# Softmax attention beside linear attention on one core: three query chunks side by side, and VectorE's exponentials split by bit masks

## The chip, the cores and the metric

The kernel runs on one core of a Trainium2 chip. The metric is the device time of one launch, in microseconds (us). The engines have queues of their own: TensorE (PE; its weight loads are PEld), VectorE (DVE), ScalarE (ACT), GpSimd (POOL) and SyncE (SP), which here issues nearly all DMAs.

## The reference

The input is one sequence of 2048 rows of 1024 features in bf16. Two layers alternate, and the pair of them is applied twice with the same weights, each with a layer norm in front and a residual around it.

```python
def _A_ref(x, wqkv, w_phi, wo):          # linear attention, 32 heads of 32
    ...
    phi_q = jnp.concatenate([_softmax(pq, axis=-1), _softmax(-pq, axis=-1)], axis=-1)
    phi_k = jnp.concatenate([_softmax(pk, axis=-1), _softmax(-pk, axis=-1)], axis=-1)
    ...
def _B_ref(x, wqkv, wo):                 # softmax attention, 32 heads of 32
    ...
    scores = jnp.einsum("bhqd,bhkd->bhqk", q, k) * (Dh ** -0.5)
    p = _softmax(scores, axis=-1)
    o = jnp.einsum("bhqk,bhkd->bhqd", p, v)
    return (lambda x, *d: x.transpose(*d))(o, 0, 2, 1, 3).reshape(B, S, D) @ wo

x = A_x
x = x + _A_ref(_layernorm(x, axis=-1), A_wqkv, A_w_phi, A_wo)
x = x + _B_ref(_layernorm(x, axis=-1), B_wqkv, B_wo)
x = x + _A_ref(_layernorm(x, axis=-1), A_wqkv, A_w_phi, A_wo)
x = x + _B_ref(_layernorm(x, axis=-1), B_wqkv, B_wo)
```

The softmax layers hold most of the work: each has 32 heads x 2048 x 2048 scores, and every one needs an exponential.

## The kernel before

The kernel keeps x transposed in SBUF (`xT`, features on the partitions) and cuts the sequence into four chunks of 512 rows (`C512`, `NC` = 4). The 32 heads are eight groups of four (`G` = 8). A **turn** of a softmax layer is one query chunk with one head group, 32 turns a layer, listed in `turns`; `pos` gives a turn its number. Within a turn there are two halves (`pp`), each with 8 steps `d` and 4 score tiles `j`: 64 tiles of 128 keys x 512 queries.

The function `attention` takes these tiles three at a time. TensorE computes three scores side by side in different row groups (L1009) into three PSUM banks, and ScalarE makes one exponential of 1536 columns of them (L1017). TensorE then multiplies the probabilities with the values and with ones, the latter for the denominators: four small matmuls (L1047) per two tiles, accumulating in bank 6 (`acc`). VectorE copies the sum out (L1062). The denominators are gathered by small DMAs on SP (L1092), inverted on VectorE (L1097), written to DRAM (L1098) and read back spread over the heads (L1100), and VectorE scales the output (L1103).

Some tiles skip ScalarE. `exp_dve` takes a *pair* of tiles: two single score matmuls (L947) into bank 7, and then nine VectorE instructions that compute 2 to the power of the score. Each score is read twice from PSUM, once to round it with a large constant (L952) and once for the fraction (L955). Two steps over both tiles make the power of two out of the rounded value (L958, L961), three multiply-adds are a polynomial of the fraction (L966), and a last one multiplies (L969). `EXTRA` says which turns have which pairs.

Everything else of the softmax layers is fill, placed between the scores, in the single PSUM bank 7 (`FIL`), and copied out by VectorE: keys (`b_k`, L842 and the DMAs of L834), values (`b_v`), queries (`b_q`, L850, with two DMAs that swap halves of the partitions in `q_swap`, L855 and L856), the output projection (`b_o` in the first layer, `b_last` in the last), and in the first softmax layer also the key features of the linear layer that follows (`a_keys`). Projections in bank 7 run as four column groups (L428). Query chunks 2 and 3 are computed early and parked in DRAM (`q_away`, L866, L868) and fetched again before their turns (`q_back`, L874 to L876).

No engine order is written out by hand. A planner on the host, `Sched`, holds every operation with an engine, an estimated duration, its dependencies, its buffers and a priority that works as a due time. It plays the engines forward and puts the operations in order; the order is then fixed in the program, and on the chip each engine goes through its own list, waiting for semaphores. `QUOTA` limits how many buffers of a class are live. `base` and `at` are the due times of a layer and of its attention; a turn is 10 units. Where TensorE would be too idle, the planner inserts idle matmuls (L1265).

Of the kernel before, what the change touches and what calls it, by code (L numbers as in the profile page):

```python
# [19 lines left out]
DH = 32  # L20
# [27 lines left out]
class Sched:  # L48
# [96 lines left out]
    def run(self):  # L145
# [25 lines left out]
        while left:  # L171
# [86 lines left out]
         "e": 6, "vp": 6, "e1": 4, "vp1": 4, "E": 6, "q2": 3, "kt": 3, "w2": 8, "w2o": 3, "oT": 26, "T": 4, "den": 2,  # L258
         "lnt": 6, "lnw": 2, "lnw1": 1, "eq": 8, "ns": 4, "cw": 6, "hl": 6, "oc": 2, "slab": 7, "slabk": 3, "fin": 4,
         "rs": 8, "pkf": 1, "cden": 2, "part": 8, "w2r": 1,  # L260
         "xs": 1, "xu": 2, "xg": 2, "xx": 2, "E1": 3}
# [3 lines left out]
ROUND = 1.5 * 2**21  # L265
POW2_D = 0.32318750170670074
POW2_0 = 0.998010015430466
POW2_C = (-2.753493604392706, 3.611980637904819, -2.738565741928622)
LEAD = 5.0
EXTRA = (lambda i: [(0, 2), (1, 2)] if 12 <= i < 17 else [],  # L270
         lambda i: ([(0, 2), (1, 2)] if i % 3 else [(0, 2), (0, 5), (1, 4)]) if 16 <= i < 30 else [(i % 2, 2)] if 8 <= i < 16 else [])
# [14 lines left out]
def kernel(  # L286
# [20 lines left out]
    q_scale = float(DH**-0.5 / (4 * math.log(2)))  # L307
# [626 lines left out]
    def exp_dve(qc, g, pp, d, prio, kT, q_of):  # L934


        u_b, u_v = sb("xu", 2, C512, dt=F32)
        g_b, g_v = sb("xg", 2, C512, dt=F32)
        x_b, x_v = sb("xx", 2, C512, dt=F32)
        e_b, e_v = sb("E1", 2, C512)  # L940
        r = slice(96, 128)
        gs = []
        for k in range(2):
            s_b, s_v = ps("xs", FIL)

            def sfn(k=k, s_v=s_v):
                nc.tensor.matmul(  # L947
                    out=s_v(), lhsT=kT[g][1]()[r, pp, (d + k) * P:(d + k + 1) * P],
                    rhs=q_of[(qc, g)][1]()[r, (pp + 1) % 2, :], start=True, stop=True, tile_position=(96, 0))
            so = op("PE", MM, sfn, flat([kT[g][2][(d + k) // 2], q_of[(qc, g)][2]]),  # L950
                    [s_b, kT[g][0], q_of[(qc, g)][0]], prio, mode="r")
            uo = op("DVE", dve_us(512), lambda k=k, s_v=s_v: nc.vector.tensor_scalar(  # L952
                out=u_v()[:, k, :], in0=s_v(), scalar1=POW2_D, scalar2=ROUND, op0=ALU.add, op1=ALU.add),
                [so], [s_b, u_b], prio + 0.01)
            gs.append(op("DVE", dve_us(512), lambda k=k, s_v=s_v: nc.vector.scalar_tensor_tensor(  # L955
                out=g_v()[:, k, :], in0=u_v()[:, k, :], scalar=ROUND, in1=s_v(), op0=ALU.subtract, op1=ALU.subtract),
                [uo], [s_b, u_b, g_b], prio + 0.01))
        wo = op("DVE", 1024 / 1920 + 0.15, lambda: nc.vector.tensor_scalar(  # L958
            out=u_v(), in0=u_v(), scalar1=ROUND - 31.5, scalar2=ROUND + 32.0, op0=ALU.max, op1=ALU.min),
            gs, [u_b], prio + 0.02)  # L960
        wo = op("DVE", 1024 / 1920 + 0.15, lambda: nc.vector.tensor_scalar(  # L961
            out=u_v().bitcast(I32), in0=u_v(), scalar1=ROUND - 31.75, scalar2=float(2**25),
            op0=ALU.subtract, op1=ALU.mult), [wo], [u_b], prio + 0.02)
        last = gs
        for i, c in enumerate(POW2_C):
            last = [op("DVE", dve_us(1024), lambda i=i, c=c: nc.vector.scalar_tensor_tensor(  # L966
                out=x_v(), in0=(x_v() if i else g_v()), scalar=c, in1=g_v(), op0=ALU.add, op1=ALU.mult),
                last, [g_b, x_b], prio + 0.02)]
        eo = op("DVE", dve_us(1024), lambda: nc.vector.scalar_tensor_tensor(  # L969
            out=e_v(), in0=x_v(), scalar=POW2_0, in1=u_v(), op0=ALU.add, op1=ALU.mult),  # L970
            [wo, *last], [x_b, u_b, e_b], prio + 0.02)
        return eo, (e_b, lambda: e_v().rearrange("p a b -> p (a b)"))

    def attention(base, kT, vT, q_of, gate, extra):
# [7 lines left out]
        for qc, g in turns:  # L982
            for pp, d in extra(pos[(qc, g)]):
                eo, (e_b, e_v) = exp_dve(qc, g, pp, d, base + 10 * pos[(qc, g)] + 5 * pp + 0.5 * d - LEAD, kT, q_of)
                for k in range(2):
                    ex_of[(qc, g, pp, d + k, 3)] = eo
                    e_of[(qc, g, pp, d + k, 3)] = (e_b, e_v, k)
# [3 lines left out]
        while i < len(units):  # L991
# [14 lines left out]
            def sfn(grp=grp, s_v=s_v):  # L1006
# [11 lines left out]
                out=e_v()[:, 0:w * C512], in_=s_v(), func=ACT.Exp, scale=4 * math.log(2)),  # L1018
# [7 lines left out]
        if True:  # L1026
            for qc, g in turns:
                T = []
                end = (qc, g) == turns[-1]
                for pp in range(2):  # L1030
                    a_b, a_v = ps("acc", [(6,)])
                    last = None
                    for d in range(8):
                        prio = base + 10 * pos[(qc, g)] + 5 * pp + 0.5 * d
                        for u in range(2):
# [4 lines left out]
                            def fn(us=us, kc=kc, u=u, d=d, a_v=a_v, v_v=v_v, g=g, pp=pp):  # L1040
                                for k in range(2):
                                    eb, ev, x = e_of[us[k]]
                                    j = 2 * pp + k
                                    for what in range(2):
                                        col = 64 * ((pp + what) % 2) + 32 * k
                                        o = (g % 4) * P + j * DH
                                        nc.tensor.matmul(  # L1047
                                            out=a_v()[col:col + 32, :],
                                            lhsT=v_v()[:, kc % 4, o:o + DH] if what == 0 else ones_bf[:],
                                            rhs=ev()[:, x * C512:(x + 1) * C512],  # L1050
                                            start=(d == 0 and u == 0), stop=(d == 7 and u == 1),
                                            tile_position=(0, col), skip_group_check=True)
# [5 lines left out]
                            last.accum = (d, u) != (7, 1)  # L1058
# [53 lines left out]
    turns = [(qc, g) for g in range(G) for qc in range(2)] + [(qc, g) for qc in range(2, NC) for g in range(G)]  # L1112
    pos = {t: i for i, t in enumerate(turns)}
# [21 lines left out]
    for layer in range(2):  # L1135
        base = BASE[layer]
        second = base + (100, 45)[layer]
# [53 lines left out]
        for g in range(1, G):  # L1191
            pr = at + 10 * pos[(0, g)] - 19
            w = slab("w2", pr - 1, B_w[:, :, D + g * P:D + (g + 1) * P], P)
            for c in range(NC):
                b_k(g, c, pr + 4 * c, w, kT, FIL, "DVE")
        for c in range(NC):
            for t in range(TB):
                b_v(1, c, t, at + 4.5 * (4 * c + t) + 2, bv_s[1], vT, FIL, "DVE")
        for g in range(G):
            pr = at + 10 * pos[(0, g)]  # L1200
            w = slab("w2", pr - 11, B_w[:, :, g * P:(g + 1) * P], P) if g else wq0
            for qc in range(NC):
                if qc < 2:
                    if qc or g:
                        q_of[(qc, g)] = b_q(g, qc, pr + 10 * qc - 8, w, FIL)
                else:
                    away = q_away(g, qc, pr + 2 + 6 * (qc - 2), w, FIL)
                    q_of[(qc, g)] = q_back(g, qc, at + 10 * pos[(qc, g)] - 12, away)
        oTs, last_s = attention(at, kT, vT, q_of, gate, EXTRA[layer])
        if last:  # L1210
            bo_s = [slab("slab", at + 160 + fc, B_o[:, :, fc * C512:(fc + 1) * C512], C512) for fc in range(2)]
        for qc, p0, gap in ((0, 163, 1.5), (1, 176, 1.5), (2, 251, 1.5)):
            if last:
                gap = (6, 6, 9)[qc]
                p0 = (163, 200, 251)[qc]
# [85 lines left out]
```

## Time and profile before

| what | value |
|---|---|
| time, median of 3 runs | 2477.9 us (2477.84 to 2481.64) |
| span of the profiled execution | 2480.3 us, clock of TensorE 0.993 |
| the profiled execution's own time | not listed apart from the span; the span is 2.4 us above the median of the runs |
| first softmax layer's attention, first to last exponential of L1017 | about 358 to 1336 us |
| second one | about 1558 to 2468 us |
| ScalarE, L1017 | 1332 exponentials, 1798.9 us |
| VectorE busy | 1380.8 us, 538 of them between 1558 and 2481 us |
| pairs on VectorE | 10 in the first layer, 40 in the second |

A row of the profile names the line, the engine, the operation, what it writes and reads, the shape and the count; then the busy time, the mean of one in ns, and the engine's idle time before it with what ended that. ScalarE's exponentials overlap: one lasts 1.67 us, but in an unbroken run they start every 1.33 to 1.35 us, which is why 1332 of them are 1798.9 us busy. TensorE's matmuls overlap in the same way.

### The profile page before, as it was taken

Reading aid. Unit: us, or ns where it says so; the run is one execution under the profiler, and the core shown is the slowest. Engines: PE = TensorE matmul, PEld = TensorE weight load, DVE = VectorE, ACT = ScalarE, POOL = GpSimd, SP = SyncE. Lnnn points to the kernel's source line nnn. Section 1 sums busy time; section 2 is a strip of 40 time slices with the busy share of each in tenths; the row PEclk is TensorE's granted clock in tenths of the full one; section 3 lists DMA queues with packets and bytes.
Section 4 is the critical chain, followed back from the end, with each engine's and each line's share of the span. In section 5 each row is a group of like instructions: output and inputs, shape, how many; then the busy total and the mean of one; then the engine's idle time right before and its main releaser. Section 6 shows DMA issues by size and latency. Waiting matters only on the chain. (4 is left out here: it accounts for less than half of the span.)

```text
span 2480.3 us, 61740 instructions
## 1 busy us (share of the span) xinstructions
PE 2316.0 (93%) x27084; PEld 870.4 (35%) x27084; DVE 1380.8 (56%) x1947; ACT 2131.0 (86%) x1887; POOL 24.9 (1%) x72
## 2 busy tenths in 40 slices
PE   7999999999999999999889999999999999998998
PEld 4443443333333333333333444333333333333333
DVE  6997653222266634543535766322255568789863
ACT  6335548999999999999997455699999999999998
POOL 0000000000000000000000000000000000000000
PEclk9999999999999999999999999999999999999999
DMA  9020011111121122213324001111121110110000
GB/s 219 24 56 1 6 38 40 43 36 45 39 66 42 47 66 70 78 50 86 120 57 128 1 5 30 31 39 43 41 61 34 31 30 29 32 32 27 27 25 32
DMA packets 204373, 118.32 MB, mean 48 GB/s; under 512 B 122440, under 2 KB 194120, under 8 KB 203336
## 3 DMA queue, kind: packets, MB, share of 16 engines
q1 hardware_dynamic: 203048, 112.29, 16.7%
q8 instruction: 211, 3.46, 0.6%
q10 hardware_dynamic: 1056, 2.10, 0.3%
q14 instruction: 58, 0.48, 0.1%
HBM read 78.71 MB, written 16.24 MB: 38 GB/s over the span
## 5 line engine op out<-in xcount | busy, mean ns | idle before, releaser
L1017 ACT ACTIVATE arena<-psum 128x1536 bf16<-128x1536 f32 x1332 | 1798.9, 1670 | 38.1 <-PE psum L1009 29.3
L1047 PE MATMUL psum<-arena 128*32 128x512 bf16 x4096 | 656.2, 388 | 7.3 <-DVE arena L1062 5.8
L1047 PE MATMUL psum<-arena,ones_bf 128*32 128x512 bf16 x4096 | 656.3, 388 | 0.0
L1009 PE MATMUL psum<-arena 32*128 32x512 bf16 x3996 | 525.0, 384 | 99.5 <-ACT arena L1017 91.1
L428 PE MATMUL psum<-arena 128*32 128x512 bf16 x8256 | 575.5, 381 | 5.4 <-DVE arena L612 1.9
L424 PE MATMUL psum<-arena 128*128 128x512 bf16 x2032 | 473.4, 382 | 17.0 <-ACT arena L745 3.2
L1009 PEld LDWEIGHTS <-arena 32*128 32x128 bf16 x3996 | 176.9, 91 | 620.6 <-issue 607.1
L424 PEld LDWEIGHTS <-arena 128*128 128x128 bf16 x2032 | 192.5, 98 | 265.4 <-issue 48.2
L428 PEld LDWEIGHTS <-arena 128*32 128x32 bf16 x8256 | 201.9, 96 | 214.8 <-issue 68.4
L1047 PEld LDWEIGHTS <-arena 128*32 128x32 bf16 x4096 | 158.0, 95 | 269.4 <-issue 238.6
L842 DVE CAST arena<-psum 128x512 bf16<-128x512 f32 x112 | 77.2, 690 | 255.2 <-PE psum L428 249.2
L966 DVE SCALAR_TENSOR_TENSOR arena<-arena 128x1024 f32<-128x1024 f32 x150 | 183.3, 1222 | 7.1 <-PE psum L1047 2.8
L1265 PE MATMUL psum<-xT,zero 128*32 128x512 bf16 x2172 | 171.7, 382 | 0.0
L1047 PEld LDWEIGHTS <-ones_bf 128*32 128x32 bf16 x4096 | 155.2, 95 | 18.7 <-issue 8.3
L1062 DVE COPY arena<-psum 128x512 f32<-128x512 f32 x126 | 86.5, 687 | 88.2 <-PE psum L1047 86.8
L615 ACT ACTIVATE arena<-psum 128x512 bf16<-128x512 f32 x80 | 42.7, 601 | 86.9 <-PE psum L424 57.5
L1103 DVE TENSOR_TENSOR arena<-arena 64x512 bf16<-64x512 f32 x124 | 84.7, 683 | 51.8 <-DMA arena<-rd 42.5
L952 DVE TENSOR_SCALAR arena<-psum 128x512 f32<-128x512 f32 x100 | 68.8, 688 | 67.7 <-PE psum L947 61.5
L745 ACT ACTIVATE arena<-psum 128x512 bf16<-128x512 f32 x128 | 69.8, 598 | 41.8 <-PE psum L424 32.0
L619 DVE TENSOR_REDUCE arena<-arena 128x32 f32<-128x1024 bf16 x64 | 77.7, 1214 | 41.2 <-ACT arena L615 34.0
L513 DVE TENSOR_TENSOR arena<-xT,arena 128x1024 f32<-128x1024 bf16 x64 | 78.0, 1219 | 35.9 <-ACT arena L502 34.7
L628 DVE TENSOR_TENSOR arena<-psum,arena 128x1024 bf16<-128x1024 f32 x64 | 77.7, 1215 | 30.0 <-PE psum L428 25.0
(100 smaller groups left out, 1394.5 us busy)
## 6 DMA issues: line engine op xcount, KB each, us to landing
arena<-rd SPq DMA_DIRECT2D x62, 256.0 KB
arena<-in_A_wqkv_dram SPq DMA_DIRECT2D x10, 1024.0 KB
arena<-in_B_wqkv_dram SPq DMA_DIRECT2D x32, 256.0 KB
arena<-arena SPq DMA_DIRECT2D x256, 32.0 KB
arena<-in_B_wo_dram SPq DMA_DIRECT2D x32, 256.0 KB
arena<-wd_k SPq DMA_DIRECT2D x8, 1024.0 KB
arena<-in_A_wo_dram SPq DMA_DIRECT2D x4, 1024.0 KB
arena<-in_B_wqkv_dram SPq DMA_DIRECT2D x4, 1024.0 KB
```

The costliest lines, as they stand in the source:

```text
L424: nc.tensor.matmul(out_, lhsT=lhsT, rhs=rhs, start=start, stop=stop, skip_group_check=True)
L428: nc.tensor.matmul(out_[ks, :], lhsT=lhsT[:, ks], rhs=rhs, start=start, stop=stop, tile_position=(0, 32 * k), skip_group_check=True)
L513: s1 = op("DVE", dve_us(1024), lambda pr=pr, w_v=w_v: nc.vector.tensor_tensor(out=w_v(), in0=xT[:, pr, csl(c)], in1=m_v().unsqueeze(1).to_ ...
L619: red = op("DVE", dve_us(1024), lambda ev=ev, sv=sv: nc.vector.reduce_sum(out=sv(), in_=ev().rearrange("p s (h d) -> p (s h) d", d=DH), ax ...
L628: ml = op("DVE", dve_us(1024), lambda vpv=vpv, wv_=wv_, sv=sv: nc.vector.tensor_tensor(out=wv_()[:, :, :, 0:DH], in0=vpv().rearrange("p (h ...
L966: last = [op("DVE", dve_us(1024), lambda i=i, c=c: nc.vector.scalar_tensor_tensor(out=x_v(), in0=(x_v() if i else g_v()), scalar=c, in1=g_ ...
L1009: nc.tensor.matmul(out=s_v()[:, x * C512:(x + 1) * C512], lhsT=kT[g][1]()[r, pp, d * P:(d + 1) * P], rhs=q_of[(qc, g)][1]()[r, (pp + j // ...
L1017: ex = op("ACT", act_us(w * C512), lambda s_v=s_v, e_v=e_v, w=w: nc.scalar.activation(out=e_v()[:, 0:w * C512], in_=s_v(), func=ACT.Exp, s ...
L1047: nc.tensor.matmul(out=a_v()[col:col + 32, :], lhsT=v_v()[:, kc % 4, o:o + DH] if what == 0 else ones_bf[:], rhs=ev()[:, x * C512:(x + 1) ...
L1062: cp = op("DVE", dve_us(512), lambda t_v=t_v, a_v=a_v: nc.vector.tensor_copy(out=t_v(), in_=a_v()), [last], [a_b, t_b], prio - 4)
L1103: s = [op("DVE", dve_us(512), lambda a=a, k=k, o_v=o_v, r_v=r_v, T=T: nc.vector.tensor_tensor(out=o_v()[a, :], in0=T[k][1]()[a, :], in1=r_ ...
L1265: nc.tensor.matmul(psum[32 * k:32 * k + 32, 6 * C512:7 * C512], lhsT=zero[:], rhs=xT[:, 0, 0:C512], start=False, stop=False, tile_position ...
```

## The change

Three things change together.

*VectorE's exponential* (`exp_dve`). The query scale now contains 2^23, so a score arrives as a number of units of the last place of a float's exponent field. One VectorE step per tile adds a bias, clamps at zero and writes an integer (the new L959); its bits are those of a float near the wanted power. A mask step splits off the fraction bits and sets the exponent to that of 1 (L962), another keeps the exponent bits alone (L965); the polynomial and the last product follow as before (L970, L973). The second read of each score from PSUM is gone. A pair is now two tiles `j` = 2, 3 of one step `d` instead of tile 3 of two steps, so its two score matmuls use different row groups.

*Order of the turns.* `SIDE` = (2, 3): in the second softmax layer, the first 24 turns go through the head groups with three query chunks each instead of two, and the last 8 turns are chunk 3. The queries of chunk 3 are computed late, about one turn ahead, from weights that are loaded again, and no chunk of that layer is parked in DRAM. Keys and values are due on a slower beat, the output blocks of chunks 0 to 2 have new due times (`OP0`, `OGAP`), all after turn 23, and their two weight slabs are loaded later and wait for a late query.

*Pairs.* The second layer has two pairs in every turn from 4 to 30, (0, 2) and (1, 4). Within a half turn, the products of VectorE's tiles are now the last of the accumulation. Some quotas change. The first layer keeps `wide` = 2 and its 10 pairs, with keys due 5 units earlier.

```diff
-         "e": 6, "vp": 6, "e1": 4, "vp1": 4, "E": 6, "q2": 3, "kt": 3, "w2": 8, "w2o": 3, "oT": 26, "T": 4, "den": 2,
+         "e": 6, "vp": 6, "e1": 4, "vp1": 4, "E": 6, "q2": 3, "kt": 3, "w2": 6, "w2o": 3, "oT": 27, "T": 4, "den": 2,
...
-         "xs": 1, "xu": 2, "xg": 2, "xx": 2, "E1": 3}
+         "xs": 1, "xu": 2, "xg": 1, "xx": 1, "E1": 3}
...
+SIDE = (2, 3)
+VGAP = 7.0
+LATE = 10.0
+BO = 225
+OP0 = (233, 259, 285)
+OGAP = (3.2, 3.2, 3.2)
 EXTRA = (lambda i: [(0, 2), (1, 2)] if 12 <= i < 17 else [],
-         lambda i: ([(0, 2), (1, 2)] if i % 3 else [(0, 2), (0, 5), (1, 4)]) if 16 <= i < 30 else [(i % 2, 2)] if 8 <= i < 16 else [])
+         lambda i: [(0,2),(1,4)] if 4<= i < 31 else [])
...
-            uo = op("DVE", dve_us(512), lambda k=k, s_v=s_v: nc.vector.tensor_scalar(
-                out=u_v()[:, k, :], in0=s_v(), scalar1=POW2_D, scalar2=ROUND, op0=ALU.add, op1=ALU.add),
-                [so], [s_b, u_b], prio + 0.01)
-            gs.append(op("DVE", dve_us(512), lambda k=k, s_v=s_v: nc.vector.scalar_tensor_tensor(
-                out=g_v()[:, k, :], in0=u_v()[:, k, :], scalar=ROUND, in1=s_v(), op0=ALU.subtract, op1=ALU.subtract),
-                [uo], [s_b, u_b, g_b], prio + 0.01))
...
+            ys.append(op("DVE", dve_us(512), lambda k=k, s_v=s_v: nc.vector.tensor_scalar(
+                out=y_v()[:, k, :].bitcast(I32), in0=s_v(), scalar1=POW2_B, scalar2=0.0, op0=ALU.add, op1=ALU.max),
+                [so], [s_b, y_b], prio + 0.01))
+        mo = op("DVE", 1024 / 1920 + 0.15, lambda: nc.vector.tensor_scalar(
+            out=m_v().bitcast(I32), in0=y_v().bitcast(I32), scalar1=0x7FFFFF, scalar2=0x3F800000,
+            op0=ALU.bitwise_and, op1=ALU.bitwise_or), ys, [y_b, m_b], prio + 0.02)
+        po = op("DVE", 1024 / 1920 + 0.15, lambda: nc.vector.tensor_scalar(
+            out=y_v().bitcast(I32), in0=y_v().bitcast(I32), scalar1=0x7F800000, scalar2=None,
+            op0=ALU.bitwise_and), [mo], [y_b], prio + 0.02)
...
+                    own = extra(pos[(qc, g)])
+                    order = [(d, u) for d in range(8) for u in range(2) if not (u and (pp, d) in own)]
+                    order += [(d, 1) for d in range(8) if (pp, d) in own]
...
+        wide = SIDE[layer]
+        turns = [(qc, g) for g in range(G) for qc in range(wide)] + [(qc, g) for qc in range(wide, NC) for g in range(G)]
...
-            pr = at + 10 * pos[(0, g)] - 19
+            pr = at + 10 * pos[(0, g)] - 24
...
+        if wide == 3:
+            for g in range(G):
+                pl = at + 10 * pos[(NC - 1, g)] - LATE
+                after = q_of[(NC - 1, g - 2) if g > 1 else (2, G - 1)][2][0]
+                wl = slab("w2", pl - 3, B_w[:, :, g * P:(g + 1) * P], P, [after])
+                q_of[(NC - 1, g)] = b_q(g, NC - 1, pl, wl, FIL)
```

## The prediction

> **What bounds the kernel now.** I read the page first, then a table of stretches, then rows inside the second attention, then the order of both built programs.
>
> From the page, the totals and the 40 slices:
>
> ```profile
> PE 2316.0 (93%) x27084; PEld 870.4 (35%) x27084; DVE 1380.8 (56%) x1947; ACT 2131.0 (86%) x1887; POOL 24.9 (1%) x72
> ...
> PE   7999999999999999999889999999999999998998
> ...
> ACT  6335548999999999999997455699999999999998
> ```
>
> TensorE looks fuller (93%), but part of that is filler: in the second attention (1558 to 2469 us) 1,420 of its matmuls are the idle ones of L1265. ScalarE reads 9 exactly in the two attention stages, and those are most of the span. The stretches of L1017 (ScalarE's exponentials; columns: stretch, busy and count, clock, DMA share, GB/s):
>
> ```profile
> 1558.00:1611.00 53.00, 28.42 (x21) 1.00 0.12 28
> 1611.00:1641.00 30.00, 28.98 (x23) 1.00 0.20 50
> 1641.00:2441.00 800.00, 798.36 (x596) 1.00 0.12 34
> ...
> 922.00:1302.00 380.00, 345.97 (x254) 0.98 0.26 76
> ```
>
> From 1641 to 2441 us ScalarE is idle for 1.6 of 800 us and retires one exponential of 1536 columns every 800/596 = 1.342 us. So the second attention runs at ScalarE's pace; only its first 83 us, where the layer before is still finishing, and its end do not. The first attention's second half (922 to 1302) is slower, 1.496 us per exponential, because ScalarE also does the next layer's key features there; the change hardly touches it.
>
> VectorE and TensorE over the second attention (groups by shape; the last figures are the mean of one in ns and the idle time before):
>
> ```profile
> L966 DVE SCALAR_TENSOR_TENSOR arena<-arena 128x1024 f32<-128x1024 f32 x120 | 146.6, 1222 | 2.4
> ...
> L952 DVE TENSOR_SCALAR arena<-psum 128x512 f32<-128x512 f32 x80 | 55.1, 689 | 55.9 <-PE psum L947 52.0 <-ACT arena L1017 2.7 <-PE psum L1009 1.1
> L955 DVE SCALAR_TENSOR_TENSOR arena<-arena,psum 128x512 f32<-128x512 f32 x80 | 55.0, 687 | 3.3
> L969 DVE SCALAR_TENSOR_TENSOR arena<-arena 128x1024 bf16<-128x1024 f32 x40 | 48.9, 1221 | 3.2 <-PE psum L1047 0.3 <-DVE arena L966 0.2 <-ACT arena L1017 0.2
> ...
> L961 DVE TENSOR_SCALAR arena<-arena 128x1024 int32<-128x1024 f32 x40 | 27.7, 693 | 1.2
> L958 DVE TENSOR_SCALAR arena<-arena 128x1024 f32<-128x1024 f32 x40 | 27.7, 693 | 1.2
> ```
>
> And what TensorE's pieces occupy, by start times in its timeline:
>
> ```profile
> 1624.44 1.04 PE L428 MATMUL psum<-arena 128*32 128x512 bf16 x16
> 1625.41 0.39 PE L1009 MATMUL psum<-arena 32*128 32x512 bf16 x3
> 1625.73 1.05 PE L428 MATMUL psum<-arena 128*32 128x512 bf16 x16
> 1626.71 0.39 PE L1009 MATMUL psum<-arena 32*128 32x512 bf16 x3
> 1627.03 0.39 PE L1047 MATMUL psum<-arena 128*32 128x512 bf16 x1
> ```
>
> Three scores take 0.32 us to the next start, and 0.11 more is lost in turning back to them: 0.43 us per score group. Sixteen projection matmuls take 0.97 with that 0.11, so a block of eight is 0.43 us. Four probability-times-value matmuls, read the same way, are 0.215 us.
>
> **The change, part by part.** *ScalarE.* In the second layer VectorE takes 2 pairs in turns 4 to 30, 54 pairs for 40, so 108 of 2048 score tiles for 80. The built program has 646 exponentials of 1536 columns and one of 1024, where there were 656: 9.33 fewer, at 1.342 us, is 12.5 us off the engine that sets the pace. The first layer keeps 10 pairs and 676 exponentials: nothing.
>
> *VectorE.* A pair cost 2 x 0.689 + 2 x 0.687 + 2 x 0.693 + 3 x 1.222 + 1.221 = 9.03 us. The second read of PSUM (L955) goes and the two clamping steps become two mask steps. If a mask costs what L958 and L961 cost, a pair is 7.65 us, and the second layer's pairs cost 54 x 7.65 = 413 us for 361. VectorE was busy 538 of 923 us there, so it would be about 65% busy. Spread over 27 turns of some 27 us it is 15.3 us a turn beside some 6 us of copies: hidden. No row shows a bit mask on integers. The bounds are 0.69 us (L961, one source, both sides in SBUF, integers out) and 1.22 us (L966, one element per cycle at the same 1024). I take 0.69, since the masks differ from L961 in the operation only. The Trainium skill ("VectorE: DVE Perf Modes", Mode 2x_2P) says that a one-source op in SBUF takes two elements per cycle even in fp32; L958 at 693 ns beside L966 at 1222 ns agrees, but no row here shows it for masks.
>
> *TensorE.* Nine score groups fewer (9 x 0.43 = 3.9 us), 28 more single score matmuls for VectorE (about 0.3 each, 8.4 us), 46 fewer idle sets. Summed over stretches of 21 score groups, the new order asks 24.3 to 26.6 us of TensorE against 27.9 us for ScalarE everywhere between the first stretch and the last 17 groups. So it stays hidden, with less filler.
>
> *Start.* In the first 42 score groups TensorE sets the pace. The order puts 56 blocks of eight there in the second layer for 68, with a few more idle sets and products: -1.8 us. In the first layer, where the keys now start earlier, it puts 72 for 68: 4 x 0.435 = +1.7 us. Together nothing.
>
> *End.* The 24 output blocks now stand in the last 8 turns instead of being spread over the second half, together with the late last queries and the 8 partial outputs. Between the last 17 score groups (16 intervals, 21.3 us at the 1.33 us that is the median spacing of the exponentials' starts) the order has 24 blocks of eight, 7 residual sets at 0.23 us, and 24 product sets: 24.3 us of TensorE, where before it was 19.3. That puts 3.0 us on the end. The tail after the last exponential (2468.2 to 2480.3 us) is the same list of instructions and stays 12 us.
>
> *Late queries.* Sixteen trips through DRAM (one write and three reads each) go; eight reloads of 256 KB and sixteen SBUF swaps come, on a DMA that is 12% busy. What matters is SP's queue: the last swap is issued behind the write of the reciprocals and the read that waits for its landing. In the trace that wait is 3.0 us from issue (2391.84 to 2394.86). The order issues the last swap at group 620 to 621 and scores need it at 626: five groups, 6.7 us, for about 4 us of issue and landing. Free, but with under 3 us to spare; before, the lead was 18 groups. The reloads and the two output slabs now also wait, in SP's queue, for a query's copy, and the reciprocals' transfers stand behind them; in the order that copy is always done when they come up. The slabs (2 MB) are issued at group 442 and first used at 464, 29 us later; at the 128 GB/s that one slice of the page reached that is 16 us.
>
> *Order within a turn.* Products of VectorE's pairs now come last in their half turn. From the last VectorE step to the product that reads it there are 7 groups or more at most pairs (9 us), but 1 to 5 at some pairs in the middle (turns 11 to 15) and near the end. With these, and product runs of five in a row, I allow 1.5 us of new ScalarE gaps (bounds 0 and 6).
>
> Sum: -12.5 + 0 + 3.0 + 1.5 = -8.0 us. The profiled span is 2480.3 us, 2.4 above the median 2477.9, so its own counterpart is 2472.3 and the predicted median 2470.
>
> **The rivals.** *Masks at one element per cycle (slower).* Each pair then costs 2 x 0.53 = 1.06 us more, 57 us in all. VectorE still has the time (647 of 911 us), but TensorE's order is fixed: where the lead is a few groups it waits for the pair, and the scores behind it wait too. Charged to the 16 pairs with least lead it is 17 us, to all 57; at about 38 the time is 2508, and from 8 us on the kernel is no faster than before. For it: integers go in as well as out, and no row covers that. Against: L961's integers cost nothing extra. The skill's same page (What auto-detection actually checks) says that the engine does not know which modes an operation has a program for, so the rate hangs on what firmware enables; that leaves this rival open rather than excluded.
>
> *The late pile-up eats the gain (no change).* Last 8 turns: 96 output blocks, 24 partial blocks and some 28 of late queries all pass through the one bank 7, as do VectorE's scores, each waiting for VectorE's copy. If each of 40 fills stalls TensorE by 0.2 us (a third of the 0.62 us that L952 waited for a score at 2060 us), that is 8 us: 2478. For it: stretches of 2.17 us between score groups near the end, over the 1.33 us of an exponential. Against: stretches as full (27 blocks per 21 groups) ran at 1.34 us early in both layers.
>
> *More than forecast.* The 1.342 us per exponential holds gaps that come from bursts on TensorE; at the median 1.33 us, 596 x 0.012 = 7 us more would go: 2463.
>
> **How the numbers follow.** My forecast has 0.60, masks 0.18, the pile-up 0.14, the larger gain 0.08. About 0.2% (5 us) is what a measurement of this kernel can tell from no change. Forecast cases lie within 6 us of 2470: most, and the larger gain, are faster than 2473; some, and the pile-up, lie within 5 us of 2478; the masks, and a bad pile-up, are slower. Faster 0.61, same 0.16, slower 0.23. The range: 2462 (the larger gain) to 2498 (the cheaper quarter of the masks' case, 2487 to 2527).
>
> **What would show it.** Right: 1,323 exponentials on ScalarE, idle under 4 us between the second attention's first 83 us and its last 25; mask steps at 0.69 us; the tail at 12 us; first attention unchanged within 2 us. Wrong: mask steps near 1.22 us; products waiting for VectorE's last step; gaps of ScalarE in the last 8 turns of more than 3 us in all; scores waiting for a swap at a late turn.

## The result, and the profile after

The changed kernel takes 2468.2 us (median of 5 runs, 2465.4 to 2471.5), the one before 2477.9 us: a ratio of 0.9958, 95% interval 0.9946 to 0.9970. The forecast was 2470 us. The two profiled executions lie further apart, at 2463.6 and 2480.3 us of span, since that of before lies at the upper end of its runs and that of after is the shortest of its five.

The page of the changed kernel, the totals and ScalarE's slices:

```profile
span 2463.6 us, 61308 instructions
...
PE 2313.0 (94%) x26908; PEld 865.8 (35%) x26908; DVE 1414.7 (57%) x1959; ACT 2118.0 (86%) x1878; POOL 24.9 (1%) x72
...
ACT  6335648999999999999997455699999999999997
```

ScalarE lost 13 us of work and VectorE gained 34. The last slice of ScalarE is 7 instead of 8. The stretches of its exponentials (L1021 now) in the second attention:

```profile
1552.00:1605.00 53.00, 28.99 (x22) 1.00 0.10 24
1605.00:1633.00 28.00, 28.00 (x22) 1.00 0.14 35
1633.00:2425.00 792.00, 790.50 (x590) 1.00 0.12 33
2425.00:2451.00 26.00, 23.06 (x18) 1.00 0.08 23
```

From 1633 to 2425 us ScalarE idles for 1.5 of 792 us and still retires one exponential per 792/590 = 1.342 us: the pace is that of before, there are only fewer to do. In the last 26 us it idles for 2.9, 0.9 of them behind its last exponential. VectorE's rows by shape (busy, mean ns of one, idle before):

```profile
L970 DVE SCALAR_TENSOR_TENSOR arena<-arena 128x1024 f32<-128x1024 f32 x162 | 197.9, 1221 | 3.6 <-PE psum L1054 0.2
...
L959 DVE TENSOR_SCALAR arena<-psum 128x512 int32<-128x512 f32 x108 | 74.5, 690 | 73.8 <-PE psum L953 67.0 <-ACT arena L1021 3.6 <-PE psum L1013 2.9
L973 DVE SCALAR_TENSOR_TENSOR arena<-arena 128x1024 bf16<-128x1024 f32 x54 | 66.1, 1224 | 3.5 <-DVE arena L970 0.2 <-ACT arena L1021 0.2
...
L962 DVE TENSOR_SCALAR arena<-arena 128x1024 int32<-128x1024 int32 x54 | 37.5, 694 | 3.6
L965 DVE TENSOR_SCALAR arena<-arena 128x1024 int32<-128x1024 int32 x54 | 37.3, 691 | 1.7
```

The two mask steps (L962, L965) cost 694 and 691 ns, and a pair 2 x 0.690 + 0.694 + 0.691 + 3 x 1.221 + 1.224 = 7.65 us, as forecast. The rule of the Trainium skill ("VectorE: DVE Perf Modes", Mode 2x_2P) that an op with one source in SBUF takes two elements per cycle holds here with integers on both sides and with two bit operations in one step.

The chain of waits at the end. Of the changed kernel, from the last scores to the first step behind them:

```profile
2448.44 0.32 PE psum L1013 x2
2448.76 0.77 PE psum L434 x24
2449.53 0.57 PE psum L1054 x9
2450.10 2.57 issue
2452.67 0.60 ACT arena L1086
```

The same place before:

```profile
2467.61 1.52 PE psum L428 x40
2469.13 0.46 PE psum L1047 x8
...
2469.68 0.60 ACT arena L1079
```

The last exponential ends at 2450.09 us after and 2468.2 before; L1086 (L1079 before) starts 2.58 and 1.44 us later. TensorE's timeline from the last scores on, after (first two lines) and before (last two):

```profile
2448.38 0.39 PE L1013 MATMUL psum<-arena 32*128 32x512 bf16 x2
...
2450.44 1.47 PE L434 MATMUL psum<-arena 128*32 128x512 bf16 x24
```

```profile
2465.60 0.39 PE L1009 MATMUL psum<-arena 32*128 32x512 bf16 x3 [0.18 <-ACT arena L1017]
...
2467.44 1.47 PE L428 MATMUL psum<-arena 128*32 128x512 bf16 x24
```

In both kernels three sets of eight output matmuls (the x24) stand on TensorE ahead of the last products; in the changed kernel they are the first 1.3 of the 2.57 us of "issue". From the last scores to the first step behind them it is 4.29 us after (2448.38 to 2452.67) and 4.08 before (2465.60 to 2469.68). What differs more is the last exponential: it has 1024 columns after and 1536 before, lasts 1.03 us for 1.91, and so ends 0.9 us earlier beside the same matmuls. From 2425 us on, the chain of the changed kernel consists of TensorE's pieces and has no exponential in it: the end is TensorE's now.

### The profile page after: what moved, and what is told of

Its sections match the earlier page's. It is cut to its first block, busy times and chain, and to the rows that moved or that the text cites. A ratio compares the mean times of both kernels' runs of the same rounds, so it can differ in the third digit from the quotient of the medians.

```text
span 2463.6 us, 61308 instructions
## 1 busy us (share of the span) xinstructions
PE 2313.0 (94%) x26908; PEld 865.8 (35%) x26908; DVE 1414.7 (57%) x1959; ACT 2118.0 (86%) x1878; POOL 24.9 (1%) x72
## 5 line engine op out<-in xcount | busy, mean ns | idle before, releaser
L1021 ACT ACTIVATE arena<-psum 128x1536 bf16<-128x1536 f32 x1323 | 1787.1, 1641 | 36.4 <-PE psum L1013 27.5
L1054 PE MATMUL psum<-arena 128*32 128x512 bf16 x4096 | 656.8, 385 | 7.3 <-DVE arena L1069 5.6
L1054 PE MATMUL psum<-arena,ones_bf 128*32 128x512 bf16 x4096 | 657.0, 386 | 0.0
L1013 PE MATMUL psum<-arena 32*128 32x512 bf16 x3968 | 533.9, 383 | 85.4 <-ACT arena L1021 76.7
L434 PE MATMUL psum<-arena 128*32 128x512 bf16 x8256 | 578.7, 381 | 4.0 <-DVE arena L523 0.7
L434 PEld LDWEIGHTS <-arena 128*32 128x32 bf16 x8256 | 205.4, 96 | 211.9 <-issue 63.2
L1054 PEld LDWEIGHTS <-arena 128*32 128x32 bf16 x4096 | 159.8, 95 | 284.1 <-issue 253.5
L970 DVE SCALAR_TENSOR_TENSOR arena<-arena 128x1024 f32<-128x1024 f32 x192 | 234.4, 1221 | 5.1 <-PE psum L1054 1.1
L1054 PEld LDWEIGHTS <-ones_bf 128*32 128x32 bf16 x4096 | 156.2, 95 | 18.4 <-issue 8.7
L1280 PE MATMUL psum<-xT,zero 128*32 128x512 bf16 x1980 | 161.4, 380 | 0.0
L959 DVE TENSOR_SCALAR arena<-psum 128x512 int32<-128x512 f32 x128 | 88.3, 690 | 86.7 <-PE psum L953 76.6
L1069 DVE COPY arena<-psum 128x512 f32<-128x512 f32 x126 | 86.5, 686 | 72.5 <-PE psum L1054 65.7
L1110 DVE TENSOR_TENSOR arena<-arena 64x512 bf16<-64x512 f32 x124 | 84.7, 683 | 51.0 <-DMA arena<-rd 43.6
L856 DVE TENSOR_SCALAR arena<-psum 128x512 bf16<-128x512 f32 x48 | 33.1, 689 | 106.9 <-PE psum L434 99.0
```

The source lines that it names most:

```text
L434: nc.tensor.matmul(out_[ks, :], lhsT=lhsT[:, ks], rhs=rhs, start=start, stop=stop, tile_position=(0, 32 * k), skip_group_check=True)
L959: ys.append(op("DVE", dve_us(512), lambda k=k, s_v=s_v: nc.vector.tensor_scalar(out=y_v()[:, k, :].bitcast(I32), in0=s_v(), scalar1=POW2_B ...
L1013: nc.tensor.matmul(out=s_v()[:, x * C512:(x + 1) * C512], lhsT=kT[g][1]()[r, pp, d * P:(d + 1) * P], rhs=q_of[(qc, g)][1]()[r, (pp + j // ...
L1021: ex = op("ACT", act_us(w * C512), lambda s_v=s_v, e_v=e_v, w=w: nc.scalar.activation(out=e_v()[:, 0:w * C512], in_=s_v(), func=ACT.Exp, s ...
L1054: nc.tensor.matmul(out=a_v()[col:col + 32, :], lhsT=v_v()[:, kc % 4, o:o + DH] if what == 0 else ones_bf[:], rhs=ev()[:, x * C512:(x + 1) ...
L1069: cp = op("DVE", dve_us(512), lambda t_v=t_v, a_v=a_v: nc.vector.tensor_copy(out=t_v(), in_=a_v()), [last], [a_b, t_b], prio - 4)
```

## The experiments

Each ratio is against the kernel before, run on the same chip beside it (its medians there were 2480.3, 2479.8 and 2479.8 us), with its 95% interval.

| run | time, us | ratio |
|---|---|---|
| after_again | 2468.3 | 0.9956 (0.9944 to 0.9969) |
| masks_alone | 2478.9 | 0.9994 (0.9985 to 1.0003) |
| two_beside | 2501.5 | 1.0085 (1.0071 to 1.0099) |
| pairs40 | 2493.1 | 1.0055 (1.0042 to 1.0067) |
| earlier_out | 2468.5 | 0.9953 (0.9940 to 0.9965) |
| late_masks | 2525.3 | 1.0188 (1.0174 to 1.0202) |
| old_steps | 2503.3 | 1.0097 (1.0083 to 1.0110) |
| pairs27 | 2494.6 | 1.0056 (1.0042 to 1.0069) |
| late_known | 2490.1 | 1.0048 (1.0036 to 1.0061) |
| pairs40_slabs | 2490.1 | 1.0041 (1.0028 to 1.0055) |
| more_first | 2461.0 | 0.9930 (0.9917 to 0.9942) |
| more_first2 | 2464.3 | 0.9939 (0.9926 to 0.9951) |

**The change as it is (after_again).** No edit; it gives a second trace.

> The changed kernel as it is, beside the kernel before, for a second profile of the same program at another granted clock. ScalarE's-pace theory (the sum of the prediction): 8 to 12 us faster than before. Rival (the first softmax layer also became faster, as the first pair of profiles shows 5 us there): a second profile shows that layer again 4 us or more shorter than in the profile of before; if the granted clock made that difference, it moves with the clock.

2468.3 us, in a profile of 2470.5 us of span. Its second attention, from the first exponential to the end of the last, lasts 899.1 us (898.0 in the first profile, 909.5 before). Its first attention lasts 975.8 us, for 972.9 in the first profile and 976.8 before, so the rival (4 us or more off that layer) is not borne out.

**VectorE's new steps alone (masks_alone).** The order of the turns, the due times, the quotas of `w2` and `oT` and the 40 pairs of before; the products of VectorE's tiles stay last in their half turn.

```diff
-SIDE = (2, 3)
-VGAP = 7.0
+SIDE = (2, 2)
+VGAP = 4.5
...
-BO = 225
-OP0 = (233, 259, 285)
-OGAP = (3.2, 3.2, 3.2)
+BO = 160
+OP0 = (163, 200, 251)
+OGAP = (6, 6, 9)
...
-         lambda i: [(0,2),(1,4)] if 4<= i < 31 else [])
+         lambda i: ([(0, 2), (1, 2)] if i % 3 else [(0, 2), (0, 5), (1, 4)]) if 16 <= i < 30 else [(i % 2, 2)] if 8 <= i < 16 else [])
...
-            pr = at + 10 * pos[(0, g)] - 24
+            pr = at + 10 * pos[(0, g)] - 19
```

> The new VectorE steps alone: pairs of two tiles of one step, bit masks, products of VectorE's tiles last in their half turn; turns, due times, quotas of w2 and oT and the 40 pairs of the second layer as before. ScalarE's-pace theory: 656 exponentials as before, VectorE's 55 us of saved work lie under ScalarE, so within 2 us of before (2478). Rival (VectorE set the pace in turns 16 to 29, where it was 85 to 90% busy): 5 us or more faster.

The interval includes 1. A pair shorter by 1.4 us is worth nothing by itself, as must be when ScalarE sets the pace. The second attention is even 3.6 us longer than before (913.1 for 909.5): one stall near 1834 us costs it 4.4 us.

**54 pairs, two chunks side by side (two_beside).** The edit above without the last but one change, so the pairs are the new 54.

> 54 pairs and the new VectorE steps, but two query chunks side by side, chunks 2 and 3 parked in DRAM, outputs and keys due as before. 647 exponentials. If ScalarE alone sets the pace: 12 us faster than before (2466), and the end without its 3 us. Rival (the three chunks are what makes room): summed over stretches of 21 score groups TensorE's order here is over ScalarE's 27.9 us by 2.2, 2.0, 4.6, 0.4, 0.5 and 1.5 us in turns 4 to 16, 11 us in all, so 2476 to 2479, no faster than before.

2501.5, over 20 us beyond what was expected. Stretches of the trace (TensorE, its loads, VectorE, ScalarE; then clock, DMA share, GB/s):

```profile
1754.00:1786.00 32.00, 31.06 (x431) 10.80 (x423) 20.35 (x27) 28.91 (x22) 0.00 (x0) 1.00 0.14 36
...
1850.00:1860.00 10.00, 4.94 (x34) 1.04 (x33) 7.82 (x9) 5.11 (x4) 0.00 (x0) 0.61 0.03 11
1860.00:1870.00 10.00, 10.00 (x107) 2.44 (x103) 7.98 (x10) 7.97 (x7) 0.00 (x0) 0.71 0.06 14
```

In the first, TensorE is 97% busy and ScalarE gets 22 exponentials in 32 us (1.45 us each). From 1720 to 1850 us the trace has 736 projection matmuls (L434) where the changed kernel has 480: with two chunks side by side a head group lasts two turns and not three, so keys and values come half again as fast, in the turns that now also hold pairs. Both have some 200 idle matmuls there (200, and 224 in the changed kernel), so not all of TensorE's time there was needed, and how much of the loss is the planner's order this run doesn't separate. At 1850 there is a stall. VectorE's timeline:

```profile
1844.27 0.69 DVE L962 TENSOR_SCALAR arena<-arena 128x1024 int32<-128x1024 int32 x1
1851.89 1.40 DVE L1110 TENSOR_TENSOR arena<-arena 64x512 bf16<-64x512 f32 x2 [6.92 <-DMA qd<-arena]
1853.33 0.69 DVE L965 TENSOR_SCALAR arena<-arena 128x1024 int32<-128x1024 int32 x1
```

VectorE stood for 6.92 us at the scaling of an output (L1110), in the middle of a pair. The trace names the store of a parked query (qd) as what ended the wait. SyncE had issued the read of the reciprocals at 1839.46, the 2 MB of output slabs at 1840.67 and that store at 1841.92 us, so both small transfers ran beside the slabs, at 320 GB/s (1844 to 1848 us).

**Three chunks side by side, 40 pairs (pairs40).** The pairs of before in the changed kernel's order.

> Three query chunks side by side and the new steps, but the 40 pairs of before in the turns of before (8 to 29). 656 exponentials. ScalarE's-pace theory: the 12.5 us come back, so 2478 to 2482, 10 to 14 us slower than the changed kernel (start -1.8, three stretches over by 3.6 us together, end -3 us against it). Rival (the order of the turns carries the gain by itself): within 4 us of the changed kernel.

2493.1 for 2478 to 2482. The excess is in two places, 2207 to 2222 and 2353 to 2375 us. At the first, SyncE's queue (the DMAs with their issue times):

```profile
2196.68 1.21 SPq L531 DMA_DIRECT2D arena<-in_B_wo_dram  x2
2197.93 4.40 SPq L531 DMA_DIRECT2D arena<-in_B_wqkv_dram  x2
2202.51 2.61 SPq L1105 DMA_DIRECT2D rd<-arena  x1
2209.05 0.59 SPq L1107 DMA_DIRECT2D arena<-rd  x1
```

The 8 KB write of the reciprocals (L1105) stands behind 2.5 MB of loads, and the read that waits for its landing is issued 6.5 us after it. In the second attention of the changed kernel that takes 1.9 us at the median of 31 times (1.4 to 4.1). What waits then, from 2196 to 2226 us (total, times, longest, in us):

```profile
PE psum L1054 <- DVE arena L1069: 7.9, 1, 7.9
...
DVE arena L1110 <- DMA arena<-rd: 7.2, 1, 7.2
...
ACT arena L1021 <- DVE arena L1110: 6.3, 1, 6.3
```

VectorE stands at L1110 for the reciprocals; the copy of the accumulator (L1069) is behind it in its queue; the products (L1054) wait for the accumulator's bank; and ScalarE, 6.3 us later, has no scores. It is the same kind of stall as in two_beside. At the second place no transfer is involved: TensorE is busy for 20.4 of 22 us, and ScalarE waits 6.3 us for its products.

**Output blocks due earlier (earlier_out).**

```diff
-OP0 = (233, 259, 285)
-OGAP = (3.2, 3.2, 3.2)
+OP0 = (230, 254, 276)
+OGAP = (3.0, 2.8, 2.8)
```

> The changed kernel with the output blocks due a little earlier and closer (233, 259, 285 with gaps 3.2 become 230, 254, 276 with gaps 3.0, 2.8, 2.8). The order then asks 19.9 us of TensorE between the last 17 score groups in place of 24.3 (21.3 us is ScalarE's), and one stretch before them is 0.1 us over. Theory (the pile-up at the end costs 3 us): 2 to 4 us faster than the changed kernel, 2465; no gap of ScalarE over 1.36 us on average in the last 38 exponentials, which were 1.40 and 1.52. Rival (the end waits for something else, such as the last copies or bank 7): the same time as the changed kernel.

The same time as the changed kernel. The end did become smooth: from the 588th exponential to the last takes 80.5 us for 82.9, and the rest after it 11.4 for 13.5. But exponentials 42 to 588 take 741.0 us for 734.5. About 4 of these 6.5 us are exponentials 525 to 588, where blocks were put; 2.7 are exponentials 273 to 336, ahead of all blocks, where the granted clock is at half for 3.4 us twice (near 1955 and 2023 us). So the blocks cost ScalarE about as much where they were put.

**Masks late, unknown to the planner (late_masks).** The mask step is issued over both tiles, one tile and both again: 1.11 us more per pair, same order.

```diff
-        po = op("DVE", 1024 / 1920 + 0.15, lambda: nc.vector.tensor_scalar(
+        def keep():
+            for k in (2, 1, 2):
+                nc.vector.tensor_scalar(
...
+        po = op("DVE", 1024 / 1920 + 0.15, keep, [mo], [y_b], prio + 0.02)
```

> The changed kernel with the last mask step of every pair done three times over (once more at 1024 columns, once at 512): 0.69 + 0.42 = 1.11 us more of VectorE for a pair, which the planner does not know, so every engine's order is that of the changed kernel. This is the price of the rival in which masks run at one element per cycle (1.06 us a pair). That rival's price was 17 to 57 us. If VectorE's spare time (35%) hides it: within 3 us of the changed kernel. If TensorE's fixed order waits wherever a pair's lead is small: 17 us or more slower, with the waits of L1054 for L973.

2525.3, 57 us above the changed kernel. The 10 pairs of the first layer are longer too; 54 x 1.11 is 60 us, and the second attention is 56 us longer (954.6 us for 898.0 and 899.1): nearly all of it arrives at the end, though VectorE has that time to spare. Not all need be the waits themselves: the granted clock is at half for 54.6 us of this attention (0.97 in the mean), and for 0 and 3.4 us in the two profiles of the changed kernel. How much of the 57 us that is, no run separates.

**The old steps in the new order (old_steps).** The nine old instructions per pair (9.03 us), with their prices known to the planner, in the changed kernel with its 54 pairs.

```diff
-            ys.append(op("DVE", dve_us(512), lambda k=k, s_v=s_v: nc.vector.tensor_scalar(
...
+            uo = op("DVE", dve_us(512), lambda k=k, s_v=s_v: nc.vector.tensor_scalar(
...
+            gs.append(op("DVE", dve_us(512), lambda k=k, s_v=s_v: nc.vector.scalar_tensor_tensor(
```

> The changed kernel with the arithmetic of before in its pairs (two reads of each score from PSUM, 9.03 us a pair for 7.65), turns, pairs and order of products as changed; the planner knows the longer steps. 647 exponentials. VectorE's 54 pairs take 488 us for 413. If the masks only make VectorE lighter and ScalarE sets the pace: the same as the changed kernel. By TensorE's stretches in this order (over by 2.7, 0.7, 0.7, 1.1 and 0.9 us, and 3.8 at the end): 6 to 8 us slower, 2475. If bank 7, held 0.69 us longer by every score, is the limit: 12 us or more slower.

2503.3, 35 us above the changed kernel, where TensorE's stretches gave 6 to 8. Only the expectation on bank 7 allows so much, but it is not shown: scores for VectorE wait 6.8 us for the second read (L961) in the whole second attention. Against the pace of 1.345 us, 9 us are lost in exponentials 210 to 252, 6.6 in 462 to 483 and, compared with the changed kernel, 20 from the 525th on. The run also keeps the changed kernel's single buffers of `xg` and `xx`, of which the old steps had two each, and the 6.6 us are a stall behind bulk loads as in pairs40. So this plan can't carry 54 pairs of the old steps; what the steps cost by themselves is not separated.

**One pair per turn (pairs27).**

```diff
-         lambda i: [(0,2),(1,4)] if 4<= i < 31 else [])
+         lambda i: [(0, 2)] if 4 <= i < 31 else [])
```

> The changed kernel with one pair a turn in turns 4 to 30: 27 pairs, 665 exponentials for 647. ScalarE's pace: 18 x 1.342 = 24 us slower, less the 3 us of the end, whose TensorE time falls to 20.6 us: 2489, 11 us slower than before. If VectorE's pairs were paid for elsewhere (bank 7, bursts on TensorE), less than that: 2475 to 2482.

2494.6 for 2489. VectorE waits for transfers three times for over 6 us here: 6.4 us at 2150, 7.1 at 2180 (for the denominators' gather, issued 6 us behind weight loads) and 6.4 at 2436 us. Where the second lies, exponentials 441 to 462 take 8.3 us more than at 1.345 us each; nowhere else behind the start is a stretch of 21 more than 1.0 us over. Less this stall, the second attention is 20 us longer than that of the changed kernel (926.7 us for 898.0), and the sum had 24 less 3. So 18 more exponentials cost their number times the spacing.

**Masks late, known to the planner (late_known).**

Against late_masks:

```diff
-        po = op("DVE", 1024 / 1920 + 0.15, keep, [mo], [y_b], prio + 0.02)
+        po = op("DVE", 1024 / 1920 + 0.15 + 1.11, keep, [mo], [y_b], prio + 0.02)
```

> The changed kernel with one more step of 1.11 us on VectorE for each pair, as in the run late_masks, but the planner's price of the step is raised by the same 1.11 us, so that the order is made for the longer pair. The run with the price unknown came out at 2525, 57 us over the changed kernel. Theory A (order): VectorE has the time (54 pairs more by 60 us on an engine that is idle for some 350 of 900 us there); what cost 57 us is products of VectorE's pairs that stand in TensorE's order before their data are there. With the price known the products stand later, and only the fuller stretches cost: 2474 to 2482. Theory B (time): VectorE's longer pair itself delays copies of the outputs and of projections whatever the order, and most of the 57 us stays: 2505 to 2525.

2490.1, between the two: of the 57 us, 35 go when the planner knows, and 22 stay. TensorE's waits from 1640 to 2460 us, first in late_masks, then in late_known:

```profile
PE psum L1057 <- DVE arena L1072: 27.7, 30, 2.1
...
PE psum L1057 <- DVE arena L976: 2.0, 2, 1.0
```

```profile
PE psum L1057 <- DVE arena L1072: 6.5, 18, 0.6
...
PE psum L1057 <- DVE arena L976: 2.0, 7, 0.5
```

With the price unknown, the products (L1057 here) wait 27.7 us for VectorE's copy of the accumulator (L1072), and only 2.0 us for the pair's own last step: the late pair holds up what is queued behind it on VectorE. Known, that is 6.5 us, and what stays lies mostly in the last 100 exponentials, where TensorE is 94% busy and ScalarE 87% (2340 to 2460 us): work was pushed into the end.

**Slabs loaded earlier (pairs40_slabs).**

```diff
-BO = 225
+BO = 205
...
-            bo_s = [slab("slab", at + BO + fc, B_o[:, :, fc * C512:(fc + 1) * C512], C512, [q_of[(2, G - 1)][2][0]])
+            bo_s = [slab("slab", at + BO + fc, B_o[:, :, fc * C512:(fc + 1) * C512], C512)
```

> The run pairs40 (three chunks side by side, but only 40 pairs on VectorE) with the load of the two 1 MB output slabs freed from the late query's copy and due 20 turns' units earlier, so that it is issued at score group 276 and not at 459. In pairs40 (2493) the first stall of some 16 us began with the reciprocals' write, which was issued 6 us behind these two loads and landed 6.5 us later. Theory A (the loads delay the small write): that stall goes, and the time is 2478 to 2486. Theory B (the stall comes from TensorE's own order at that place, the loads only coincide): 2490 to 2496, with a gap of 5 us or more between two exponentials at the same turn.

The stall at 2207 us is gone: the write of 2206.5 is followed by its read at 2209.0, and exponentials 462 to 483 take 1.348 us each for 1.777, 9 us less. But 2490.1 is only 3 us less, because the planner's order changed too: exponentials 357 to 420 now take 1.475, 1.664 and 1.400 us, 11 us more, with 40 idle matmuls in a row between two score groups at 2087 us. So the stall went with the loads, as theory A has it; since the order changed as well, the total can't confirm it.

**More pairs in the first layer (more_first, more_first2).**

```diff
-EXTRA = (lambda i: [(0, 2), (1, 2)] if 12 <= i < 17 else [],
+EXTRA = (lambda i: [(0, 2), (1, 4)] if 10 <= i < 17 else [(0, 2)] if 17 <= i < 20 or 28 <= i < 31 else [],
```

and in the second of them

```diff
+EXTRA = (lambda i: [(0, 2), (1, 4)] if 10 <= i < 19 else [(0, 2)] if 28 <= i < 31 else [],
```

> The changed kernel with more of the first layer's pairs on VectorE: two in each of turns 10 to 16 and one in turns 17 to 19 and 28 to 30, where the changed kernel has two in turns 12 to 16 only. ScalarE does 670 exponentials of 1536 columns in that layer for 676. Theory A (ScalarE sets the pace there too): 6 x 1.342 = 8 us less than the changed kernel, 2460. Theory B (in the first layer's second half TensorE and the bank that takes VectorE's scores and the next layer's keys set the pace): the same as the changed kernel or up to 8 us more, 2468 to 2476.

> As more_first, but two pairs in each of turns 10 to 18 and one in turns 28 to 30: 669 exponentials in the first layer for 676, and nearly all of the additional pairs stand where the next layer's keys are not yet being made. Theory A (ScalarE's pace): 7 x 1.342 = 9 us less than the changed kernel, 2459. Theory B (TensorE and the shared bank are full there): 2468 to 2476. If this one gains and more_first does not, the late turns of the first layer are what is full.

2461.0 and 2464.3: the first is faster than the changed kernel (0.9930, interval to 0.9942, beside 0.9956, from 0.9944), by some 7 us for the 8 expected; the second by some 4 for 9, and its interval meets that of the changed kernel. From the first exponential to the end of the last, their first attention takes 971.5 and 966.2 us, where the six profiles with the same steps, keys and 10 pairs have 971.5 to 975.8; more_first's has the granted clock at half for 10 us near 720 us. The second run gains in the first attention and loses in the second: 903.3 us for 898.0 and 899.1, with four spells of 3.4 us at half clock in it (none and one in those); around three of them a stretch of 21 exponentials is 1.0 to 1.6 us over its pace. So by the totals ScalarE's pace is worth having in the first layer too, and the late turns are not what is full; the 3 us between the two runs may be the clock alone. more_first is the fastest version found.

## Why the prediction was right

**ScalarE, -12.5 us.** Right. Exponentials 42 to 588 of the second attention take 734.6 us before and 734.5 after, 1.345 us each; nine fewer are 12.1 us. more_first takes six more off ScalarE and gains some 7 us.

**Masks at 0.69 us.** Right, 0.694 and 0.691. The rival that they take 1.22 falls. Its price had been 17 to 57 us by how many pairs are caught late; late_masks, with 1.11 us on each pair, came out at the upper end, part of it perhaps the clock. (The rival's 57 us leave out the 10 pairs of the first layer.) The reason that I gave (a product waits for its pair) holds for only 2.0 us of it in that run; the copy of the accumulator behind the pair is the larger part.

**Start.** Right: the first 42 exponentials take 82.2 us before and 80.5 after in the second layer (-1.7 for -1.8), and in the first, by the stretches of 21, 1.7 us more (2.613 and 1.376 us each for 2.499 and 1.415), as forecast.

**End, +3.0 us.** Right in size, at 3.8 us. From the 588th exponential on, one takes 82.9/59 = 1.405 us for 92.7/68 = 1.363 before: 2.4 us. Another 1.4 us are in the tail, 13.5 us for 12.1, which I had said would stay 12. But 0.9 of these only move from one to the other, since the last exponential is shorter; counted from starts, the exponentials give 3.3 us (81.9/58 for 90.8/67) and the tail, from the start of the last, 0.5 (14.6 for 14.0). So the sign of a 12 us tail failed, and the cost stands where the prediction had it, on TensorE among the last scores. My mark for a wrong forecast, gaps of more than 3 us in the last 8 turns, is just met (3.0 us, and 4.3 in after_again): the mark repeated a cost that the sum already held.

**New gaps, +1.5 us.** Nearer to its lower bound: 0 in the middle (1.1 in after_again, where a spell of 3.4 us at half clock falls at 2308 us). No late swap delayed a score in the last turns; the one wait for a DMA by a score of VectorE's is 1.4 us, at 1950 us.

The measured terms are -12.1 - 1.7 + 1.7 + 2.4 + 1.4 = -8.3 us for the -8.0 of the sum. The medians lie 9.7 apart, and 12.0 beside after_again, so 1 to 4 us are outside these terms and unexplained. The two profiles' other 8 us can't be put down to the change: most of them are in the first attention after its 400th exponential, 413.7 us before and 407.1 after, where masks_alone, with the order of before, took 406.9. In those 400 us the profile of before shows four stretches of 50 us at a clock of 0.97, that of after two. The sign that the first attention stays within 2 us thus fails in the first profile (3.9 shorter) and holds in the second (1.0). One plain consequence: the pair of profiles alone would have said 17 us.

**The late pile-up.** It is real (the end and the tail, 3.8 us) but was not the larger thing, and earlier_out shows that moving it a little earlier gains nothing.

**More than forecast.** Falls: the pace is 1.342 us after as before, so its small gaps stayed.

What my sum did not see is how narrow the case was. The new steps alone give 0; steps and pairs without the order +21, steps and order without the added pairs +13, order and pairs without the new steps +23 us against the kernel before. My expectations for two of these (two_beside, pairs40) missed by 11 to 25 us, by stalls that no sum over TensorE's work holds.

A long wait of VectorE for a transfer does not always cost: it waits 8.3 us at 2443 us in two_beside, 8.2 at 2393 in masks_alone and 6.3 at 2422 in the kernel before, and ScalarE's exponentials run on unbroken beside each. The waits that do cost have something in common. In SyncE's queue the transfer stands close behind the 2 MB of output weights, in pairs40, pairs27 and old_steps with some other weights between:

| run | output weights issued, us | the transfer behind them, us | VectorE waits, us | ScalarE idles in the next 30 us |
|---|---|---|---|---|
| masks_alone | 1825.0 | a query's store, 1826.3 | 8.5 | 4.0 |
| two_beside | 1840.7 | a query's store, 1841.9 | 6.9 | 8.5 |
| pairs40 | 2196.7 | write of the reciprocals, 2202.5 | 7.2 | 8.5 |
| pairs27 | 2167.2 | gather of denominators, 2175.8 | 7.1 | 7.7 |
| old_steps | 2197.3 | read of the reciprocals, 2203.0 | 4.9 | 6.3 |

In the changed kernel the next small transfer is issued 9.7 us behind these weights (2169.4 and 2179.0 us), in pairs40_slabs 10.1 us, and ScalarE idles for 0.0 us. In the kernel before a gather follows after 3.3 us, and nothing waits for it, so distance alone does not decide. The prediction had priced these loads by their first use, 29 us later, and not by what stands behind them. Whether the changed order keeps its distance by design or by luck of the planner is open.

## What to carry to other kernels

Price an edit at the engine that sets the pace: here the number of exponentials times their spacing, less what the end costs, gave the result within 2 us, while the parts that fed it were worth nothing alone. An engine that is 57% busy still works in order, so a longer step or an early wait for a transfer on it delays whatever is queued behind, and a planner must know both durations. Put small round trips through DRAM ahead of bulk loads in a queue, or the bulk well before them.

## What the runs showed of the hardware

A write of 8 KB behind 2.5 MB of loads from the same queue took 6.5 us until its reader could be issued (pairs40), 2.5 us where the 2 MB of output weights had been loaded long before (pairs40_slabs). The Trainium skill ("DMA: Bandwidth & Descriptors", Queues, rings and completion order) has it that each DMA engine takes a queue's descriptors in order and that the completion signal lands only behind the earlier writes of that engine; the two runs agree with that.

After these stalls TensorE does not come back at full speed. Two_beside, by 4 us:

```profile
1848.00:1852.00 4.00, 1.54 (x23) 0.51 (x16) 0.11 (x1) 0.41 (x1) 0.00 (x0) 1.00 0.52 170
1852.00:1856.00 4.00, 1.76 (x11) 0.40 (x14) 3.90 (x5) 3.27 (x3) 0.00 (x0) 0.53 0.00 0
1856.00:1860.00 4.00, 3.17 (x27) 0.64 (x19) 3.81 (x5) 1.85 (x2) 0.00 (x0) 0.50 0.02 4
1860.00:1864.00 4.00, 4.00 (x31) 0.66 (x27) 2.14 (x4) 3.26 (x3) 0.00 (x0) 0.50 0.15 34
1864.00:1868.00 4.00, 4.00 (x49) 1.18 (x50) 3.90 (x5) 2.90 (x2) 0.00 (x0) 0.76 0.00 0
```

The granted clock (third number from the right) halves as the stall ends and stays there for some 14 us, six of them with TensorE fully busy. Over these rows and the 4 us ahead of them ScalarE is idle for 8.3 of 24 us, for a wait of 6.9 on VectorE. The same number is 0.57 from 2210 to 2220 us in pairs40. A stall is not needed for it: the second attention of the kernel before has two spells of 3.4 us at half clock, at 2093 and 2390 us, with no wait of ScalarE over 1 us.
